# A block-sparse attention and SoLU kernel: moving VectorE's mask words into a PSUM bank, narrowing the masks, and merging TensorE's mask products

## The chip, the cores and the metric

The kernel runs on one core of a Trainium2 chip, as one launch. The metric is device time in microseconds (us). Before the change the median of three runs is 208.88 us (207.01 to 212.43). One further execution was profiled. It took 206.78 us, of which 205.1 us lie between the first and the last profiled instruction (the span).

## What is computed

The inputs are q, k and v of shape (4 batches, 8 heads, 768 tokens, 64), a table of three sampled key blocks for each of the 24 query blocks of 32 tokens, and the three weights of a feed-forward layer (512 to 1024 to 512). Cut to what matters:

```
scores = scale * q @ k.T                               # per batch and head, 768 x 768
mask   = |blk_i - blk_j| <= 1  or  blk_i in (0, 23)  or  blk_j in (0, 23)  or  blk_j in sampled[blk_i]
attn   = softmax(where(mask, scores, -1e9))
x      = attn @ v                                      # heads side by side: 3072 x 512
h      = x @ w_in                                      # 3072 x 1024
solu   = h * softmax(h)
out    = layer_norm(solu) * g_ln @ w_out               # 3072 x 512
```

The first and the last query block see every key. So the mask is all true in the rows of these two blocks, whatever was sampled.

## The kernel before, in words

**Tiling.** The scores are made transposed: keys on the 128 partitions, queries along the free axis. Tokens are dealt out to chunks of 128 so that a chunk holds every second token of the first 256 (chunks 0 and 1) or every fourth token of the other 512 (chunks 2 to 5). In a chunk of the first kind a block of 32 tokens is 16 neighbouring columns, in one of the second kind 8. The first query block is thus the first 16 columns of the first two query chunks, and the last query block is the last 8 columns of the last four.

A **pass** `ps` is one batch and one pair of query chunks (`j` = 0, 1, 2): 12 passes. In a pass there are four pairs of heads and, for each, three **units** `s`, each with two key chunks: 144 units in all. A unit is the work between two steps of this chain:

- `score_one` (L719): TensorE writes scores of two heads x two key chunks x 256 queries to `sco`, a pair of PSUM banks, of which there are two. TensorE works as two halves of 64 rows, called T0 and T64 in the plan: half `t` makes the scores of head `t` and owns bank `t` of the pair.
- `exps` (L740): ScalarE takes the exponential of the whole pair of banks (128 x 1024) into `exs` in SBUF.
- the mask, in one of three ways, picked by a letter in the string `MASK` (L254) for each unit. For `P` (52 units: 19 with j = 0 and 33 with j > 0) TensorE adds a product `sel x mrow` to the scores, so that masked scores are very negative: one more 256-column product for each of the two key chunks and each half, four in a unit. For `V` (28 units: 9 with j = 0 and 19 with j > 0) VectorE, and for `G` (64 units: 20 and 44) GpSimd, clears the masked values of `exs` after the exponential, in `mask_out` (L711): one instruction of 128 x 512 int32 words, each word two bf16 values, against the tile `seenV` or `seenG`, which is broadcast over heads, key chunks and query chunks. These tiles lie in SBUF and hold 64 words for each of the four cases (first key chunks or later ones, first query chunks or later ones).
- `outs_one` (L748): TensorE multiplies `exs` by V into `op`: 16 products of 65 columns in a unit, 8 for each half (the 65th column is the softmax sum). `op` is one PSUM bank, of which 2 x 2 x 65 = 260 of the 512 fp32 columns are used. Products of the two halves must not write one bank at the same time, so `half_mm` (L341) puts a wait between the last product of one half and the first of the other.
- `normalise` (L759), after three units: VectorE takes reciprocals of the sums and writes the normalised output to `xb`. The next pair of heads uses `op` after that.

After a pass, `xb` is transposed, `h_one` multiplies by w_in into the banks `h0` and `h1`, ScalarE takes exponentials (`e_half`, L840), VectorE multiplies (`solu_half`, L848), makes statistics, and after a transposing DMA `o_one` multiplies by w_out into the bank `o`. With `sco` 2 x 2, `op`, `h0`, `h1` and `o`, all 8 banks of PSUM are used.

**Order of the work.** All of this is put down as jobs by `at` (L474), with planned durations (`D_MUL` for VectorE's mask, `D_MULG` for GpSimd's, `D_SC` for one score product). `LANES` (L355) holds, by hand, the order of the jobs for each engine: T0, T64, A (ScalarE), V (VectorE), G (GpSimd), SP (DMA queue). `emit` (L481) plays the jobs through in planned time and then issues all instructions in order of planned start. So the order on VectorE, ScalarE, GpSimd and SP is the written one. TensorE has one queue, into which T0 and T64 are merged by planned start, part by part: products of different jobs interleave there, and an instruction that waits holds all behind it. `port=True` on a job says that VectorE and GpSimd may not run at the same time in the plan. The semaphores between engines are put in by the framework, from which tile each instruction reads and writes, in the order in which they are issued.

**Other lines that the change touches.** `turn_pe` (L663), `x_turn_pe` (L780) and `ln_turn_pe` (L863) use the `op` bank for transposes in the prologue and at the end. `seen_mm` (L1118) makes the mask of the four cases in a PSUM tile, and `seen_put` (L1126) turns it into `seenG` and `seenV`, with one VectorE instruction for each.

Of the kernel before, what the change touches and what calls it, by code (L numbers as in the profile page):

```python
# [8 lines left out]
FP32 = mybir.dt.float32  # L9
BF16 = mybir.dt.bfloat16  # L10
I32 = mybir.dt.int32
AX = mybir.AxisListType
ALU = mybir.AluOpType
# [196 lines left out]
def kernel(  # L210
# [11 lines left out]
    nc = tc.nc  # L222

    B, H, S, D = q.shape
# [3 lines left out]
    TQ = 128  # L228
# [7 lines left out]
    KD = d_model // 128  # L236
    KF = d_ff // 128
# [4 lines left out]
    PC = 2  # L242
    QW = PC * TQ
# [12 lines left out]
            "PGPGVPVVPGPGGVPPGGPVGGGGGGVVGGPVGGGGGPGGPVGGPGGP")  # L256

    D_SC, D_PV, D_O, D_EXP, D_EH = 109.5, 31.2, 216, 905, 565
    D_SOLU, D_NORM, D_MUL, D_BN, D_ST, D_OT, D_RS = 675, 640, 670, 610, 570, 750, 560
    D_MULG = 1360  # L260
    PE_LAT, X_LAT = 170, 75
    HALT = 95
    UNIT = 1313.47
# [50 lines left out]
    fix = work.enter_context(tc.tile_pool(name="fix", bufs=1))  # L314
# [4 lines left out]
    QT = [fix.tile([TQ, NP, NCH, TQ], BF16, name=f"QT{i}") for i in range(2)]  # L319
    sel = fix.tile([TQ, 2, TQ], BF16, name="sel")  # L320
    mrow = fix.tile([TQ, 2, TQ], BF16, name="mrow")
    seen = {e: fix.tile([TQ, 2, 2, TQ // 2], I32, name=f"seen{e}") for e in "GV"}
    VA = [fix.tile([TQ, H, NCH, D + 1], BF16, name=f"VA{i}") for i in range(2)]

    a_st = work.enter_context(tc.tile_pool(name="a_st", bufs=8))
# [6 lines left out]
    p_op = work.enter_context(tc.tile_pool(name="p_op", bufs=1, space=bass.MemoryType.PSUM))  # L332
    p_h = work.enter_context(tc.tile_pool(name="p_h", bufs=1, space=bass.MemoryType.PSUM))
    p_o = work.enter_context(tc.tile_pool(name="p_o", bufs=1, space=bass.MemoryType.PSUM))

    SYNC = mybir.DependencyInfo(mybir.DependencyClass.Sync, mybir.DependencyReason.DATA)
    held = {}
# [323 lines left out]
    def turn_pe(b, pr, key, c0, c1, pool):  # L663
        if pool == "h0":
            tp = p_h.tile([TQ, 1024], BF16, tag="h0", name=f"tp_{key}{b}_{pr}_{c0}")
        elif pool == "h1":
            tp = p_h.tile([TQ, 1024], BF16, tag="h1", name=f"tp_{key}{b}_{pr}_{c0}")
        elif pool == "op":
            tp = p_op.tile([TQ, 1024], BF16, tag="op", name=f"tp_{key}{b}_{pr}_{c0}")
        else:  # L670
            tp = p_o.tile([TQ, 1024], BF16, tag="o", name=f"tp_{key}{b}_{pr}_{c0}")
        turned[key, b, pr, c0] = tp
        for c in range(c0, c1):
            nc.tensor.matmul(tp[:, (c - c0) * TQ : (c - c0 + 1) * TQ],  # L674
                             nat[key, b, pr, c0][:, c].rearrange("p h d -> p (h d)"), ident,
                             is_transpose=True, start=(c == c0), stop=(c == c1 - 1))
# [18 lines left out]
    box = {}  # L695
    L = NPASS - 1
    exs_of, sco_of, op_of, xb_of = {}, {}, {}, {}

    def unit(s):
        ps, r = divmod(s, SLOTS)  # L700
        pr, u = divmod(r, UP)
        b, j = divmod(ps, NPB)
        return ps, b, j, pr, u

    def by_product(s):
        return MASK[s] == "P"

    def n_scores(s):
        return 4 if by_product(s) else 2

    def mask_out(eng, s):  # L711
        ps, b, j, pr, u = unit(s)
        e = exs_of[ps, pr][:, u].bitcast(I32).rearrange("p a b (c t) -> p (a b c) t", c=PC)
        m = seen[eng][:, int(u > 0), int(j > 0)].rearrange("p (o t) -> p o t", o=1)
        (V if eng == "V" else G).tensor_tensor(  # L715
            out=e, in0=e, in1=m.broadcast_to([TQ, 4 * PC, TQ // 2]),
            op=ALU.bitwise_and if eng == "V" else ALU.mult)

    def score_one(s, t, n):  # L719
        ps, b, j, pr, u = unit(s)  # L720
        if s not in sco_of:
            sco_of[s] = p_sco.tile([TQ, 2, 512], FP32, tag="sco", name=f"sco{s}")
        m, kk = divmod(n, 2)
        p = slice(t * D, (t + 1) * D)
        c = 2 * u + kk
        if m == 0:
            kt = KT[b % 2][p, pr, c, :]
            qt = QT[b % 2][p, pr, PC * j : PC * (j + 1), :].rearrange("p c t -> p (c t)")
        else:
            kt = sel[p, int(u > 0), :]  # L730
            qt = mrow[p, int(j > 0)].rearrange("p (o t) -> p o t", o=1).broadcast_to([D, PC, TQ])
        nc.tensor.matmul(sco_of[s][:, t, kk * QW : (kk + 1) * QW], kt, qt, start=(n == 0),  # L732
                         stop=(n == n_scores(s) - 1), skip_group_check=True)

    def scores(s):
        for n in range(n_scores(s)):
# [11 lines left out]
    def outs_one(s, t, n):  # L748
        ps, b, j, pr, u = unit(s)
        if (ps, pr) not in op_of:  # L750
            op_of[ps, pr] = p_op.tile([TQ, 2, PC, D + 1], FP32, tag="op", name=f"op{s}")
        op, exs = op_of[ps, pr], exs_of[ps, pr]
        r = slice(t * D, (t + 1) * D)
        hh, ic, kk = n >> 2, n >> 1 & 1, n & 1
        half_mm(("op", ps, pr), t, 16 * UP, op[:, hh, ic, :],
                exs[r, u, hh, kk, ic * TQ : (ic + 1) * TQ],
                VA[b % 2][r, 2 * pr + hh, 2 * u + kk, :])
# [20 lines left out]
                                    in_=xb_of.pop(ps).rearrange("p c m -> p (c m)"))  # L778

    def x_turn_pe(ps):  # L780
        pool, tag = (p_op, "op") if ps == L else (p_o, "o")
        box["tpx"] = tp = pool.tile([128, PC * KD, 128], BF16, tag=tag, name=f"tpx{ps}")
        xb = xb_of.pop(ps).rearrange("p c (k e) -> p (c k) e", e=128)
        for c in range(PC * KD):
            nc.tensor.matmul(tp[:, c, :], xb[:, c, :], ident, is_transpose=True,
                             start=(c == 0), stop=(c == PC * KD - 1))
        xT_of[ps] = [mo_sb.tile([128, KD, 128], BF16, tag=f"lnT_{i}", bufs=3,
                                name=f"xT{ps}_{i}")
                     for i in range(PC)]
# [71 lines left out]
    tpl_of = {}  # L861

    def ln_turn_pe(ps, i, a, z):  # L863
        t = ps * PC + i
        if a == 0:
            lnT_of[ps, i] = [mo_sb.tile([128, KF // 2, 128], BF16, tag=f"lnT_{a}",
                                        bufs=3, name=f"lnT{t}_{a}") for a in range(2)]
            tpl_of[ps, i] = p_op.tile([128, KF, 128], BF16, tag="op", name=f"tpl{t}")
        for c in range(a, z):
            nc.tensor.matmul(tpl_of[ps, i][:, c, :], solu_of[ps, i][:, c * 128 : (c + 1) * 128],  # L870
                             ident, is_transpose=True, start=(c == 0), stop=(c == KF - 1))
# [85 lines left out]
    with tc.manual_schedule():  # L957
        V, G, A = nc.vector, nc.gpsimd, nc.scalar
# [59 lines left out]
        for r in range(NR):  # L1018
            V.tensor_scalar(out=planes[:, r + 1], in0=io_f, scalar1=samp_f[:, r : r + 1],
                            scalar2=NEG, op0=ALU.not_equal, op1=ALU.mult)  # L1020
# [103 lines left out]
                                     stop=(kk + kq == 2), skip_group_check=True)  # L1124

        def seen_put(eng):  # L1126
            V.tensor_scalar(out=seen[eng], in0=box["seen"], scalar1=-0.5,
                            scalar2=1.0 if eng == "G" else -1.0, op0=ALU.is_ge, op1=ALU.mult)

        at(2.6, "T0", seen_mm, dur=140, lat=PE_LAT + X_LAT, reads=[("M", 1)], out="sn",  # L1130
           bank=("o", "sn"))
# [48 lines left out]
        for s in range(n_units):  # L1180
# [16 lines left out]
            if not by_product(s):  # L1197
                eng = MASK[s]
                at(s + A_MUL, eng, mask_out, eng, s, dur=D_MUL if eng == "V" else D_MULG,
                   reads=[("E", s), "seen"], out=("X", s), port=eng == "V")  # L1200
                got = ("X", s)
            for t in range(2):
                if True:
# [7 lines left out]
        for b in range(1, B):  # L1211
            s0 = SLOTS * NPB * (b - 1) + (L1 if b == 1 else L2)
            n = 0
# [220 lines left out]
```

## Time and profile before

| what | value |
|---|---|
| median of three runs | 208.88 us (207.01 to 212.43) |
| profiled execution, its own time | 206.78 us |
| its span, first to last instruction | 205.1 us |
| granted TensorE clock | 1.00 |
| busy share of the span: TensorE, ScalarE, VectorE, GpSimd | 95%, 85%, 77%, 71% |

How to read it. PE is TensorE, PEld its weight loads, DVE VectorE, ACT ScalarE, POOL GpSimd, SP the queue that issues DMAs. The chain that ended last is followed back from the last instruction, at each step to what released it or to the instruction before it on its engine; its shares say which engine set the end. A group is one line of code on one engine, with its count, busy time, mean duration, and the idle time before it with what ended that. `half_mm`'s line, L346, stands for most products, so these are told apart by the tile that they write: `op`, `h`, `o`, `tpx`. The ends of products are modelled: a record of an `op` product lasts 0.19 us although the next one starts 0.03 us later. Where cost on TensorE matters, the distance between starts is read, not the duration.

### The profile page before, as it was taken

To read this page: it belongs to the slowest core of one execution; us is meant where nothing else is said; L and a number is where in the kernel's file an instruction comes from. 1 tells how busy PE (TensorE), PEld (TensorE's weight loads), DVE (VectorE), ACT (ScalarE), POOL (GpSimd) and SP (SyncE) were. 2 spreads that over 40 slices of the span, in tenths; PEclk is the share of its full clock that TensorE was granted. 3 is DMA by queue.
4 is the path that set the end of the run, shared out by engine and by line. 5 is a ranking of instruction groups with operands and counts; after the bars stand their busy time and mean duration, and the time that the engine had idled before them with its cause. 6 is when DMAs were issued, how large, how long until landed. Compare 5 with 4: busy or idle time off the path is not lost.

```text
span 205.1 us, 9410 instructions
## 1 busy us (share of the span) xinstructions
PE 195.0 (95%) x4052; PEld 153.5 (75%) x4052; DVE 157.6 (77%) x374; ACT 173.8 (85%) x254; POOL 145.9 (71%) x165
## 2 busy tenths in 40 slices
PE   7899899999999999999899999999999999999992
PEld 2478677778888788887777989888788687886451
DVE  3375644899887877978579898898988978777992
ACT  4589887998998989989799999899989889883481
POOL 6497677788866978977877769798689578651211
PEclk9999999999999999999999999999999999999999
DMA  5999998565798999999999999999976225503543
GB/s 163 333 336 277 294 367 240 122 104 118 178 211 185 245 258 253 249 164 209 144 238 272 248 223 254 214 264 159 170 200 178 54 54 157 107 0 66 167 183 109
DMA packets 74977, 39.84 MB, mean 194 GB/s; under 512 B 46900, under 2 KB 71732, under 8 KB 74932
## 3 DMA queue, kind: packets, MB, share of 16 engines
q1 hardware_dynamic: 73204, 37.50, 81.8%
q0 software_dynamic: 528, 1.05, 2.7%
q8 instruction: 32, 0.52, 1.1%
q10 hardware_dynamic: 1200, 0.66, 1.1%
q14 instruction: 13, 0.11, 0.2%
HBM read 23.07 MB, written 6.29 MB: 143 GB/s over the span
## 4 chain that ended last, share of the span: by engine, by line
PE 71%; DMA 14%; SPq 4%; POOL 4%; issue 2%; ACT 2%; DVE 1%; ACTq 0%; POOLq 0%
PE op L346 22%; PE sco L732 19%; PE h L346 12%; PE o L346 9%; DMA lnT<-solu 5%; DMA st_q<-in_q_dram 4%; DMA KT<-n_k 3%; DMA st_k<-in_k_dram 2%; SPq L641 2%; PE h L812 2%; POOL exs L715 2%; POOL n_q L622 1%; PE o L913 1%; PE tp_k L674 1%; PE tp_q L674 1%
## 5 line engine op out<-in xcount | busy, mean ns | idle before, releaser
L744 ACT ACTIVATE exs<-sco 128x1024 bf16<-128x1024 f32 x144 | 140.8, 1029 | 13.3 <-PE sco L732 11.9
L715 POOL TENSOR_TENSOR exs<-exs,seenG 128x512 int32<-128x512 int32 x64 | 81.7, 1288 | 23.6 <-ACT exs L744 23.6
L346 PE MATMUL op<-VA,exs 64*128 64x65 bf16 x2304 | 95.6, 190 | 1.2 <-issue 0.8
L346 PEld LDWEIGHTS <-exs 64*128 64x128 bf16 x2304 | 86.6, 94 | 10.8 <-issue 1.9
L732 PE MATMUL sco<-QT,KT 64*128 64x256 bf16 x576 | 81.5, 272 | 1.2 <-DMA KT<-n_k 0.8
L346 PE MATMUL h<-w_in_sb,xT 64*128 64x512 bf16 x352 | 82.5, 376 | 0.0
L346 PE MATMUL o<-w_cen_sb,lnT 64*128 64x512 bf16 x320 | 80.7, 376 | 0.3 <-DMA lnT<-solu 0.3
L732 PEld LDWEIGHTS <-KT 64*128 64x128 bf16 x576 | 38.8, 94 | 8.5 <-issue 1.9
L853 DVE TENSOR_TENSOR solu<-h,e 128x512 bf16<-128x512 f32 x48 | 32.6, 684 | 4.7 <-ACT e L844 4.4
L844 ACT ACTIVATE e<-h 128x512 bf16<-128x512 f32 x48 | 28.8, 601 | 8.5 <-PE h L346 4.4
L346 PEld LDWEIGHTS <-xT 64*128 64x128 bf16 x352 | 29.7, 93 | 5.3 <-issue 1.1
L346 PEld LDWEIGHTS <-lnT 64*128 64x128 bf16 x320 | 29.0, 93 | 4.7 <-issue 0.7
L882 DVE BATCH_NORM_STATS2 stats<-solu 128x6 f32<-128x512 bf16 x48 | 31.4, 681 | 0.1
L732 PE MATMUL sco<-mrow,sel 64*128 64x256 bf16 x208 | 28.1, 276 | 0.9 <-issue 0.9
L900 POOL TENSOR_TENSOR rstd<-vpe,mhalf 128x1 f32<-128x1 f32 x24 | 14.9, 623 | 16.7 <-DVE vpe L893 16.7
L715 DVE TENSOR_TENSOR exs<-exs,seenV 128x512 int32<-128x512 int32 x28 | 23.8, 858 | 1.7 <-ACT exs L744 1.6
L765 DVE RECIPROCAL recip_all<-op 128x4 f32<-128x4 f32 x48 | 8.6, 180 | 19.2 <-PE op L346 18.0
L766 DVE TENSOR_TENSOR xb<-op,recip_all 128x256 bf16<-128x256 f32 x48 | 20.4, 424 | 1.7
L622 POOL CAST n_q<-st_q 128x768 bf16<-128x768 f32 (+2 forms) x19 | 15.7, 843 | 4.3 <-DMA st_q<-in_q_dram 4.3
L939 DVE TENSOR_SCALAR ot<-o,rstd 128x512 f32<-128x512 f32 x20 | 14.9, 745 | 4.0 <-PE o L346 3.1
L732 PEld LDWEIGHTS <-sel 64*128 64x128 bf16 x208 | 15.4, 96 | 2.5 <-issue 1.4
L622 POOL CAST VA<-st_v 128x768 bf16<-128x768 f32 x16 | 13.6, 856 | 3.8 <-DMA st_v<-in_v_dram 3.8
(79 smaller groups left out, 133.4 us busy)
## 6 DMA issues: line engine op xcount, KB each, us to landing
out_dram<-ot SPq DMA_DIRECT2D x10, 512.0 KB, 4.0
st_k<-in_k_dram SPq DMA_DIRECT2D x16, 256.0 KB, 5.1
st_v<-in_v_dram SPq DMA_DIRECT2D x16, 256.0 KB, 4.7
st_q<-in_q_dram SPq DMA_DIRECT2D x16, 256.0 KB, 4.5
st_k<-in_k_dram SPq DMA_DIRECT2D x16, 128.0 KB, 4.9
st_v<-in_v_dram SPq DMA_DIRECT2D x16, 128.0 KB, 3.9
wf<-in_moe_w_out_dram SPq DMA_DIRECT2D x4, 512.0 KB, 9.7
st_q<-in_q_dram SPq DMA_DIRECT2D x12, 128.0 KB, 4.5
```

The source lines that it names most:

```text
L346: i = nc.tensor.matmul(out, lhsT, rhs, start=(n == 0), stop=(n == n_all - 1), skip_group_check=True, is_transpose=turn)
L622: eng.tensor_copy(out=out, in_=in_)
L715: (V if eng == "V" else G).tensor_tensor(out=e, in0=e, in1=m.broadcast_to([TQ, 4 * PC, TQ // 2]), op=ALU.bitwise_and if eng == "V" else AL ...
L732: nc.tensor.matmul(sco_of[s][:, t, kk * QW : (kk + 1) * QW], kt, qt, start=(n == 0), stop=(n == n_scores(s) - 1), skip_group_check=True)
L744: nc.scalar.activation(out=exs_of[ps, pr][:, u].rearrange("p a b c -> p (a b c)"), in_=sco_of.pop(s).rearrange("p a b -> p (a b)"), func=A ...
L765: nc.vector.reciprocal(out=recip, in_=op[:, :, :, D : D + 1])
L766: nc.vector.tensor_tensor(out=xb_of[ps][:, :, 2 * pr * D : 2 * (pr + 1) * D].rearrange("p c (h d) -> p h c d", h=2), in0=op[:, :, :, 0:D], ...
L844: nc.scalar.activation(out=e_of[ps, i][:, half * HF : (half + 1) * HF], in_=h_bank(ps, i, half), func=ACT.Exp, scale=1.0, accum_out=eh_all ...
L853: nc.vector.tensor_mul(out=solu_of[ps, i][:, c], in0=h_bank(ps, i, half), in1=e_of[ps, i][:, c])
L882: nc.vector.bn_stats(out=st_of[ps, i][:, half, :], in_=solu_of[ps, i][:, half * HF : (half + 1) * HF])
L900: nc.gpsimd.tensor_tensor(out=rstd_of[ps, i], in0=stat_of.pop((ps, i)), in1=mhalf, op=ALU.pow)
L939: eng.tensor_scalar(out=o, in0=i, scalar1=rs, scalar2=None, op0=ALU.mult)
```

## The change

Four things are changed.

- **Where VectorE's mask words lie.** The `op` bank becomes one tile, `op_bank`, that is taken once and kept for the whole kernel. The accumulators `op`, and the transposes that used the bank, become views of it. `seenV` in SBUF goes; its words lie in columns 260 to 499 of `op_bank` as `seen_v`. `seenG` stays in SBUF as `seen_g`.
- **Narrower masks.** `some(j)` gives the columns that still need a mask: 16 to 127 of each chunk for j = 0, and 0 to 119 for j > 0. The instruction of VectorE and of GpSimd thus has 8 x 56 = 448 or 8 x 60 = 480 words instead of 512. `seen_put` writes `seen_v` in two instructions, one for j = 0 and one for j > 0.
- **One mask product per half.** For `P` units the two products of 256 columns for each half become one that covers both key chunks, of 4 x 112 = 448 or 4 x 120 = 480 columns. The selector is the same for both key chunks, so nothing is lost.
- **The plan's numbers.** `D_MUL` goes from 670 to 640, `D_MULG` from 1360 to 1170, a `P` unit has three parts instead of four, and VectorE's mask job no longer excludes GpSimd. `MASK` and `LANES` are unchanged.

```diff
--- before.py
+++ after.py
@@ -256,8 +256,8 @@
             "PGPGVPVVPGPGGVPPGGPVGGGGGGVVGGPVGGGGGPGGPVGGPGGP")
 
     D_SC, D_PV, D_O, D_EXP, D_EH = 109.5, 31.2, 216, 905, 565
-    D_SOLU, D_NORM, D_MUL, D_BN, D_ST, D_OT, D_RS = 675, 640, 670, 610, 570, 750, 560
-    D_MULG = 1360
+    D_SOLU, D_NORM, D_MUL, D_BN, D_ST, D_OT, D_RS = 675, 640, 640, 610, 570, 750, 560
+    D_MULG = 1170
     PE_LAT, X_LAT = 170, 75
     HALT = 95
     UNIT = 1313.47
@@ -319,7 +319,7 @@
     QT = [fix.tile([TQ, NP, NCH, TQ], BF16, name=f"QT{i}") for i in range(2)]
     sel = fix.tile([TQ, 2, TQ], BF16, name="sel")
     mrow = fix.tile([TQ, 2, TQ], BF16, name="mrow")
-    seen = {e: fix.tile([TQ, 2, 2, TQ // 2], I32, name=f"seen{e}") for e in "GV"}
+    seen_g = fix.tile([TQ, 2, 2, TQ // 2], I32, name="seen_g")
     VA = [fix.tile([TQ, H, NCH, D + 1], BF16, name=f"VA{i}") for i in range(2)]
 
     a_st = work.enter_context(tc.tile_pool(name="a_st", bufs=8))
@@ -334,6 +334,11 @@
     p_o = work.enter_context(tc.tile_pool(name="p_o", bufs=1, space=bass.MemoryType.PSUM))
 
 
+
+    op_bank = p_op.tile([TQ, 512], FP32, name="op_bank")
+    OPW = 2 * PC * (D + 1)
+    MW = TQ // 2 - 4
+    seen_v = op_bank[:, OPW : OPW + 4 * MW].bitcast(I32).rearrange("p (k j q) -> p k j q", k=2, j=2)
 
     SYNC = mybir.DependencyInfo(mybir.DependencyClass.Sync, mybir.DependencyReason.DATA)
     held = {}
@@ -666,7 +671,7 @@
         elif pool == "h1":
             tp = p_h.tile([TQ, 1024], BF16, tag="h1", name=f"tp_{key}{b}_{pr}_{c0}")
         elif pool == "op":
-            tp = p_op.tile([TQ, 1024], BF16, tag="op", name=f"tp_{key}{b}_{pr}_{c0}")
+            tp = op_bank.bitcast(BF16)
         else:
             tp = p_o.tile([TQ, 1024], BF16, tag="o", name=f"tp_{key}{b}_{pr}_{c0}")
         turned[key, b, pr, c0] = tp
@@ -706,31 +711,42 @@
         return MASK[s] == "P"
 
     def n_scores(s):
-        return 4 if by_product(s) else 2
+        return 3 if by_product(s) else 2
+
+    def some(j):
+        return (TQ // 8, TQ) if j == 0 else (0, TQ - TQ // 16)
 
     def mask_out(eng, s):
         ps, b, j, pr, u = unit(s)
+        a, z = some(j)
         e = exs_of[ps, pr][:, u].bitcast(I32).rearrange("p a b (c t) -> p (a b c) t", c=PC)
-        m = seen[eng][:, int(u > 0), int(j > 0)].rearrange("p (o t) -> p o t", o=1)
+        e = e[:, :, a // 2 : z // 2]
+        kk, kq = int(u > 0), int(j > 0)
+        m = seen_v[:, kk, kq, 0 : (z - a) // 2] if eng == "V" else seen_g[:, kk, kq, a // 2 : z // 2]
         (V if eng == "V" else G).tensor_tensor(
-            out=e, in0=e, in1=m.broadcast_to([TQ, 4 * PC, TQ // 2]),
+            out=e, in0=e, in1=m.rearrange("p (o t) -> p o t", o=1).broadcast_to(
+                [TQ, 4 * PC, (z - a) // 2]),
             op=ALU.bitwise_and if eng == "V" else ALU.mult)
 
     def score_one(s, t, n):
         ps, b, j, pr, u = unit(s)
         if s not in sco_of:
             sco_of[s] = p_sco.tile([TQ, 2, 512], FP32, tag="sco", name=f"sco{s}")
-        m, kk = divmod(n, 2)
         p = slice(t * D, (t + 1) * D)
-        c = 2 * u + kk
-        if m == 0:
+        o = sco_of[s][:, t, :]
+        if n < 2:
+            c = 2 * u + n
             kt = KT[b % 2][p, pr, c, :]
             qt = QT[b % 2][p, pr, PC * j : PC * (j + 1), :].rearrange("p c t -> p (c t)")
+            o = o[:, n * QW : (n + 1) * QW]
         else:
+            a, z = some(j)
             kt = sel[p, int(u > 0), :]
-            qt = mrow[p, int(j > 0)].rearrange("p (o t) -> p o t", o=1).broadcast_to([D, PC, TQ])
-        nc.tensor.matmul(sco_of[s][:, t, kk * QW : (kk + 1) * QW], kt, qt, start=(n == 0),
-                         stop=(n == n_scores(s) - 1), skip_group_check=True)
+            qt = mrow[p, int(j > 0), a:z].rearrange("p (o t) -> p o t", o=1).broadcast_to(
+                [D, 2 * PC, z - a])
+            o = o.rearrange("p (c t) -> p c t", t=TQ)[:, :, a:z]
+        nc.tensor.matmul(o, kt, qt, start=(n == 0), stop=(n == n_scores(s) - 1),
+                         skip_group_check=True)
 
     def scores(s):
         for n in range(n_scores(s)):
@@ -748,7 +764,7 @@
     def outs_one(s, t, n):
         ps, b, j, pr, u = unit(s)
         if (ps, pr) not in op_of:
-            op_of[ps, pr] = p_op.tile([TQ, 2, PC, D + 1], FP32, tag="op", name=f"op{s}")
+            op_of[ps, pr] = op_bank[:, 0:OPW].rearrange("p (h c e) -> p h c e", h=2, c=PC)
         op, exs = op_of[ps, pr], exs_of[ps, pr]
         r = slice(t * D, (t + 1) * D)
         hh, ic, kk = n >> 2, n >> 1 & 1, n & 1
@@ -778,8 +794,11 @@
                                     in_=xb_of.pop(ps).rearrange("p c m -> p (c m)"))
 
     def x_turn_pe(ps):
-        pool, tag = (p_op, "op") if ps == L else (p_o, "o")
-        box["tpx"] = tp = pool.tile([128, PC * KD, 128], BF16, tag=tag, name=f"tpx{ps}")
+        if ps == L:
+            tp = op_bank.bitcast(BF16).rearrange("p (c t) -> p c t", t=128)
+        else:
+            tp = p_o.tile([128, PC * KD, 128], BF16, tag="o", name=f"tpx{ps}")
+        box["tpx"] = tp
         xb = xb_of.pop(ps).rearrange("p c (k e) -> p (c k) e", e=128)
         for c in range(PC * KD):
             nc.tensor.matmul(tp[:, c, :], xb[:, c, :], ident, is_transpose=True,
@@ -865,7 +884,7 @@
         if a == 0:
             lnT_of[ps, i] = [mo_sb.tile([128, KF // 2, 128], BF16, tag=f"lnT_{a}",
                                         bufs=3, name=f"lnT{t}_{a}") for a in range(2)]
-            tpl_of[ps, i] = p_op.tile([128, KF, 128], BF16, tag="op", name=f"tpl{t}")
+            tpl_of[ps, i] = op_bank.bitcast(BF16).rearrange("p (c t) -> p c t", t=128)
         for c in range(a, z):
             nc.tensor.matmul(tpl_of[ps, i][:, c, :], solu_of[ps, i][:, c * 128 : (c + 1) * 128],
                              ident, is_transpose=True, start=(c == 0), stop=(c == KF - 1))
@@ -1124,8 +1143,15 @@
                                      stop=(kk + kq == 2), skip_group_check=True)
 
         def seen_put(eng):
-            V.tensor_scalar(out=seen[eng], in0=box["seen"], scalar1=-0.5,
-                            scalar2=1.0 if eng == "G" else -1.0, op0=ALU.is_ge, op1=ALU.mult)
+            if eng == "G":
+                V.tensor_scalar(out=seen_g, in0=box["seen"], scalar1=-0.5, scalar2=1.0,
+                                op0=ALU.is_ge, op1=ALU.mult)
+                return
+            for kq in range(2):
+                a, z = some(kq)
+                V.tensor_scalar(out=seen_v[:, :, kq, 0 : (z - a) // 2],
+                                in0=box["seen"][:, :, kq, a // 2 : z // 2], scalar1=-0.5,
+                                scalar2=-1.0, op0=ALU.is_ge, op1=ALU.mult)
 
         at(2.6, "T0", seen_mm, dur=140, lat=PE_LAT + X_LAT, reads=[("M", 1)], out="sn",
            bank=("o", "sn"))
@@ -1197,7 +1223,7 @@
             if not by_product(s):
                 eng = MASK[s]
                 at(s + A_MUL, eng, mask_out, eng, s, dur=D_MUL if eng == "V" else D_MULG,
-                   reads=[("E", s), "seen"], out=("X", s), port=eng == "V")
+                   reads=[("E", s), "seen"], out=("X", s), port=False)
                 got = ("X", s)
             for t in range(2):
                 if True:
```

## The prediction

> **What bounds the kernel now.** I read the page first: busy shares, the chain that ended last, and the costly groups.
>
> ```profile
> PE 195.0 (95%) x4052; PEld 153.5 (75%) x4052; DVE 157.6 (77%) x374; ACT 173.8 (85%) x254; POOL 145.9 (71%) x165
> ...
> PE 71%; DMA 14%; SPq 4%; POOL 4%; issue 2%; ACT 2%; DVE 1%; ACTq 0%; POOLq 0%
> ...
> L744 ACT ACTIVATE exs<-sco 128x1024 bf16<-128x1024 f32 x144 | 140.8, 1029 | 13.3 <-PE sco L732 11.9
> L715 POOL TENSOR_TENSOR exs<-exs,seenG 128x512 int32<-128x512 int32 x64 | 81.7, 1288 | 23.6 <-ACT exs L744 23.6
> ...
> L715 DVE TENSOR_TENSOR exs<-exs,seenV 128x512 int32<-128x512 int32 x28 | 23.8, 858 | 1.7 <-ACT exs L744 1.6
> ```
>
> TensorE is the bound: 71% of the chain is its own work, and where ScalarE idles before an exponential it waits for TensorE's scores (11.9 of 13.3 us). VectorE has 1% of the chain and GpSimd 4%. Next, busy time by stage, and the chain's shares by line:
>
> ```profile
> 40.00:80.00 40.00, 40.00 (x903) 32.83 (x898) 33.56 (x75) 37.56 (x55) 31.64 (x34) 1.00 0.93 187
> ```
>
> ```profile
> by line: PE op L346 22.4%; PE sco L732 18.7%; PE h L346 11.7%; PE o L346 9.3%; DMA lnT<-solu 4.7%; DMA st_q<-in_q_dram 4.3%; DMA KT<-n_k 3.0%; DMA st_k<-in_k_dram 2.1%; SPq L641 2.1%; issue 2.0%; PE h L812 1.7%; POOL exs L715 1.6%; POOL n_q
> ```
>
> In the middle of the kernel TensorE (first pair of numbers) is busy for 40.00 of 40 us and ScalarE (fourth) for 37.56. Neither has much to give back: a hole in TensorE's work there is mostly lost.
>
> **Part 1: the mask words in op's bank.** The question is what happens when VectorE reads columns 260 to 499 of a bank while TensorE accumulates in columns 0 to 259. Before, no mask touches that bank, so the two overlap freely. Whether the program lets two engines touch one bank at once, I read at the end of the kernel, where it has two such cases. First, the two halves of `tpx` are copied out by two engines into two different tiles:
>
> ```profile
> 187.97 0.75 DVE L939 TENSOR_SCALAR ot<-o,rstd 128x512 f32<-128x512 f32 x1
> ...
> 187.98 0.62 PE L785 MATMUL tpx<-ident,xb 128*128 128x128 bf16 x8
> ...
> 188.63 0.58 ACT L620 COPY xT<-tpx 128x512 bf16<-128x512 bf16 x1
> ...
> 189.25 0.42 DVE L622 COPY xT<-tpx 128x512 bf16<-128x512 bf16 x1 [0.52 <-ACT xT L620]
> ```
>
> VectorE was free at 188.72 and `tpx` finished at 188.60, yet its copy starts at 189.25, 0.04 us after ScalarE's copy of the other half ended. Second, `tpl` is written in two halves by TensorE:
>
> ```profile
> 194.18 0.39 PE L870 MATMUL tpl<-ident,solu 128*128 128x128 bf16 x4
> ...
> 195.03 0.58 ACT L620 COPY lnT<-tpl 128x512 bf16<-128x512 bf16 x1
> ...
> 195.66 0.38 PE L870 MATMUL tpl<-ident,solu 128*128 128x128 bf16 x4 [0.22 <-ACT lnT L620]
> ```
>
> The second half, other columns, waits for ScalarE's copy of the first (end 195.61) and starts 0.05 us later. So in this program engines take turns on one PSUM tile, even on disjoint columns. `op_bank` makes accumulators and mask words one such tile. I conclude that each V mask will wait for the `op` products issued ahead of it, and the `op` products issued behind it will wait for the mask; behind those, in TensorE's one queue, everything else waits too: scores (and so ScalarE), `h`, `o`. The Trainium skill, "PSUM — Partial Sum Buffer", section "PSUM bank collisions raise a hardware error", states the rule behind such waits: two engines on one bank and the same 32 partitions collide whichever columns they touch, so semaphores must guard by bank, not by address. The two waits above agree with it. By that rule the sum below stands; if only shared columns had to be ordered, the second rival's sum would.
>
> How often do the two meet? I took a stretch of 0.64 us (the new mask's length, below) from the start of each of the 28 V masks, and asked how long `op` products run in it:
>
> ```profile
> 12.83:13.47 0.64, 0.54 (x18) 0.00 (x0) 1.00 1.08 327
> ...
> 21.40:22.04 0.64, 0.09 (x3) 0.09 (x1) 1.00 1.23 208
> ...
> 29.91:30.55 0.64, 0.00 (x0) 0.00 (x0) 1.00 1.13 341
> ...
> 174.02:174.66 0.64, 0.58 (x19) 0.00 (x0) 1.00 0.00 0
> sum 17.92, PE 11.43 DVE 0.49; mean PE 0.41 DVE 0.02
> ```
>
> Sixteen stretches are like the first and the last, with `op` at work for over 0.5 us from the start on; eight have between 0.09 and 0.41 us (1.96 us in all); four have at most 0.01. One of the sixteen, and what a hand-over costs:
>
> ```profile
> 73.84 0.47 PE L346 MATMUL op<-VA,exs 64*128 64x65 bf16 x10
> ...
> 74.10 0.68 DVE L715 TENSOR_TENSOR exs<-exs,seenV 128x512 int32<-128x512 int32 x1
> ...
> 74.24 0.23 PE L346 MATMUL op<-VA,exs 64*128 64x65 bf16 x2
> ```
>
> ```profile
> L346 PE MATMUL op<-VA,exs x2304: 187/191/202, 12.4 to 186.9; 64*128 64x65 bf16 x192
> ```
>
> ```profile
> 13.93 0.41 PE L346 MATMUL op<-VA,exs 64*128 64x65 bf16 x8
> ...
> 14.37 0.18 DVE L765 RECIPROCAL recip_all<-op 128x4 f32<-128x4 f32 x1 [0.65 <-PE op L346]
> ```
>
> Ten products whose records span 0.47 us start 0.03 us apart. In the hand-over to VectorE the reciprocal starts 0.03 us after the last record ends, so about 0.23 us after that product's start (0.19 + 0.03). So a mask in mid-burst costs TensorE's queue 0.23 (product to mask) + 0.64 (mask) + 0.05 (mask to product, as with `tpl`) less the usual 0.03: 0.89 us. Sixteen are 14.2 us. The eight partial ones cost at least the product time that is pushed behind the mask, 1.96, and 0.05 each: 2.4. Sum 16.6 us. Bounds: 11.4 (only the overlap in the sum row is pushed back) and 28 x 0.92 = 25.8 (every mask in mid-burst). What of it reaches the end? The chain is TensorE's for 71%; the rest is DMA and others, under which a hole is hidden. 0.71 x 16.6 = **+11.8 us**. VectorE's own wait lies beside its idle time (23% of the span), but `solu_half` and `normalise` are queued behind it, which I leave to the upper bound.
>
> **Part 2: what the masks cost by themselves.** No mask with a PSUM operand is in the trace. The nearest row is the product of `h` (PSUM) with `e` (SBUF); a smaller one gives the slope.
>
> ```profile
> L853 DVE TENSOR_TENSOR solu<-h,e x48: 672/681/693, 33.7 to 197.3; 128x512 bf16<-128x512 f32 x48
> ```
>
> ```profile
> L715 POOL TENSOR_TENSOR exs<-exs,seenG x64: 1259/1268/1779, 16.7 to 183.8; 128x512 int32<-128x512 int32 x64
> L715 DVE TENSOR_TENSOR exs<-exs,seenV x28: 672/701/1556, 12.8 to 174.0; 128x512 int32<-128x512 int32 x28
> ```
>
> ```profile
> L766 DVE TENSOR_TENSOR xb<-op,recip_all 128x256 bf16<-128x256 f32 x48 | 20.4, 424 | 1.7
> ```
>
> (681 - 424) / 256 = 1.0 ns a column: 448 columns take 617 ns and 480 take 649; with 9 and 19 masks the mean is 0.64 us. The old mask has a tail (median 701, most 1556) and so has GpSimd's (1268, 1779), while `solu`, which reads one operand from PSUM, has none. So I take the tail as gone: 28 x (858 - 640) = 6.1 us of VectorE. GpSimd's mask goes by columns from its shortest: 1102 and 1180, mean 1156 with 20 and 44; 64 x (1288 - 1156) = 8.4 us. VectorE's gain lies beside TensorE's work (1% of the chain) and counts nothing; if that cover went, it would be up to 6.1. Of GpSimd's 81.7 us, 1.6% of the span, 3.3 us, lie on the chain; a tenth of that is saved: **-0.3 us**, bounds 0 and -3.3.
>
> **Part 3: one mask product per half.**
>
> ```profile
> 29.26 0.27 PE L732 MATMUL sco<-QT,KT 64*128 64x256 bf16 x1
> ...
> 29.37 0.27 PE L732 MATMUL sco<-QT,KT 64*128 64x256 bf16 x1
> ...
> 29.48 0.27 PE L732 MATMUL sco<-mrow,sel 64*128 64x256 bf16 x1
> ...
> 29.59 0.27 PE L732 MATMUL sco<-mrow,sel 64*128 64x256 bf16 x1
> ```
>
> Products of 256 columns start 0.11 us apart: 0.42 ns a column. With j = 0 a unit saves 64 columns (27 ns) in each half, with j > 0, 32 (13 ns). The halves run side by side, so one counts: 19 x 27 + 33 x 13 = 0.94 us, times 0.71: **-0.7 us**. The 104 instructions that go away are worth at most 0.03 us each, the distance of `op` starts: 3.1 us as the bound; other work starts in between, so I take nothing for them.
>
> **Part 4: the rest.**
>
> ```profile
> L1127 DVE TENSOR_SCALAR seenV<-seen_ps 128x256 int32<-128x256 f32 x1 | 0.4, 412 | 0.0
> ```
>
> ```profile
> L622 DVE CAST mrow<-m_ps 128x128 bf16<-128x128 f32 x2 | 0.6, 285 | 0.2 <-PE m_ps L1028 0.2
> ```
>
> `seen_put` for VectorE becomes two instructions of 112 and 120 columns; by the 128-column cast they take up to 0.57 us instead of 0.41. This one time, 0.16 us is hidden under TensorE's prologue; uncovered it costs 0.16. The changed numbers of the plan move where T0's and T64's products interleave; the plan counts the merged product as 109.5 ns, by the rows above it is 0.19 to 0.20. I give this 0, with 1 us to either side.
>
> **The sum.** 206.8 (profiled execution) + 11.8 - 0.3 - 0.7 = 217.6 us. The median of the runs before is 2.1 us above the profiled one, so a median after may lie between 217.6 and 219.7; I say **218.5**. The likeliest case's own range goes with 7.5 to 17 us of added time: 213 to 225.
>
> **Rivals.**
>
> - *The holes grow.* Each V mask ties three engines in a row: TensorE waits for the mask, the mask for the exponential, the exponential for scores that TensorE makes. For it: ScalarE's 37.56 of 40 us leave little to catch up. Against it: two `sco` buffers. All 16.6 us count, and in the four idle and eight partial stretches the masks move into bursts too (25.8 at most): 206.8 + 16.6 to 25.8 - 1 gives 222 to 232, middle 227. Chance 0.17.
> - *No turns are taken, not slower.* Accumulators and mask words are views of one tile, but are ordered only where columns overlap. Place: the same 28 masks; price: zero instead of 16.6. It decides as soon as TensorE starts `op` products during a mask. Then only the gains are left: -0.3 - 0.7, with up to -3.3 and -3.1 as bounds: 203 to 206, middle 205.5. For it: the prologue and the end are the only places where the trace shows turns. Against it: both show them on disjoint columns. Chance 0.13, of which faster by over 2% 0.04.
> - *VectorE waits, not TensorE.* If the order of issue puts most masks just behind a burst of `op`, TensorE loses little and VectorE's waits (28 x about 0.5 = 14 us) go into its 47 idle us. For it: four stretches without `op`. Against it: sixteen with. 206.8 + 2.4 to 6, less 1: 208 to 212. Chance 0.15, half of it within 2%.
> - *The forecast*: chance 0.55.
>
> 2%, 4.1 us, is about what a measurement of this kernel can tell from no change. Slower by more: 0.55 + 0.17 + 0.07 = 0.79. Faster by more: 0.04. Within: 0.17. The range for 8 in 10 reaches from the lower end of the third rival, 208, to just past the middle of the first, 228; what lies outside is the second rival (0.13) and a tail of the first.
>
> **What would show it.** Right: among the waits, VectorE's masks wait for `op` products, and `op` products or their weight loads wait for `exs` L715, some 24 times and 0.5 to 0.9 us each; in the stretch of a mask no `op` product starts; ScalarE's wait for `sco` grows from 11.9 us by a similar sum; V masks take 0.62 to 0.65 us without tail, GpSimd's mean falls to about 1.16 us; merged products, half as many, are followed 0.19 to 0.20 us later by the next of their half. Wrong: `op` products that start while a mask reads the bank; or the waits are there and the time is not, because TensorE catches up.

## The result and the profile after

The kernel after takes 221.51 us (median of six runs, 221.0 to 222.1), the kernel before 209.26 us (six runs, 207.01 to 212.43). The ratio is 1.0626, with a 95% interval of 1.0561 to 1.069: slower by 12.3 us. Medians are over all runs and ratios over the fast ones: some runs of the kernel before, and of the kernels below that come out like it, are over 1.5% slower than their fastest, so a loss taken from medians is a little too small (between medians of fast runs it is 12.6 us here, and 14.0 where 13.4 is named below). The forecast was 218.5 us in a range of 208 to 228, slower with a chance of 0.79. The profiled execution after took 221.24 us, with a span of 219.7 us.

First the page after, with the rows that answer to those of before: busy time, the chain by engine and by line, and the groups of ScalarE's exponential, of `op`'s products (now `op_bank`) and of the two kinds of mask.

```profile
PE 197.3 (90%) x3948; PEld 150.3 (68%) x3948; DVE 153.3 (70%) x375; ACT 174.9 (80%) x254; POOL 134.1 (61%) x165
...
PE 82%; DVE 9%; ACT 2%; DMA 2%; issue 2%; SPq 0%; DVEq 0%; ACTq 0%
PE op_bank L351 29%; PE sco L748 19%; PE h L351 13%; PE o L351 11%; DVE exs L726 7%; DMA st_k<-in_k_dram 2%; PE h L831 2%; PE tpx L351 1%; PE o L932 1%; PE tp_q L679 1%; ACT exs L760 1%; PE mean_ps L1184 1%; PE oo L932 1%; PE tp_k L679 1%; DVE xb L782 1%
...
L760 ACT ACTIVATE exs<-sco 128x1024 bf16<-128x1024 f32 x144 | 141.1, 1027 | 22.8 <-PE sco L748 20.2
L351 PE MATMUL op_bank<-VA,exs 64*128 64x65 bf16 x2304 | 97.0, 190 | 13.5 <-DVE exs L726 13.4
L726 POOL TENSOR_TENSOR exs<-exs,seen_g 128x480 int32<-128x480 int32 (+1 forms) x64 | 75.0, 1181 | 51.1 <-ACT exs L760 51.1
...
L726 DVE TENSOR_TENSOR exs<-exs,op_bank 128x480 int32<-128x480 int32 (+1 forms) x28 | 17.9, 640 | 11.5 <-PE op_bank L351 10.7
```

Every engine's share of the span has fallen: all wait more. TensorE's busy time has even grown, from 195.0 to 197.3 us, with 104 products fewer. All of VectorE was 1% of the chain; now its mask alone is 7% of the span on it (15 us). The idle time ahead of `op` products was 1.2 us before and is 13.5 us now, and 13.4 of it ends with VectorE's mask. ScalarE's wait for scores has grown from 11.9 to 20.2 us.

The waits say it in both directions. The columns are the total in us, the number of times, and the longest.

```profile
ACT exs L760 <- PE sco L748: 20.2, 29, 1.6
PEld L351 <- issue: 19.6, 28, 1.2
...
PE op_bank L351 <- DVE exs L726: 13.4, 21, 0.8
DVE exs L726 <- PE op_bank L351: 10.7, 20, 1.2
```

The busy time of `op` products (and of the few transposes in that bank) inside the V masks, each cut by 0.02 us at its start and to 0.58 us:

```profile
13.17:13.75 0.58, 0.00 (x0) 1.00 1.13 317
...
186.66:187.24 0.58, 0.00 (x0) 1.00 0.91 184
sum 16.23, PE 0.00; mean PE 0.00
```

Before, 11.43 of 17.92 us of mask time had `op` products under it. Now it is 0.00 of 16.23, in all 28. The two never run at once. TensorE as a whole does not always stand: with other products it is busy for 6.21 of these 16.23 us; in 12 of the 28 masks it does nothing.

One of the turns from near, the same unit that the prediction showed at 74.10 us:

```profile
77.57 0.36 PE L748 MATMUL sco<-mrow,sel 64*128 64x480 bf16 x1
...
77.77 0.63 PE L351 MATMUL op_bank<-VA,exs 64*128 64x65 bf16 x15
...
78.51 0.66 DVE L726 TENSOR_TENSOR exs<-exs,op_bank 128x480 int32<-128x480 int32 x1 [0.25 <-PE op_bank L351]
79.22 0.19 PE L351 MATMUL op_bank<-VA,exs 64*128 64x65 bf16 x1 [0.82 <-DVE exs L726]
...
79.23 0.39 PE L351 MATMUL h<-w_in_sb,xT 64*128 64x512 bf16 x1
...
79.25 0.38 PE L748 MATMUL sco<-QT,KT 64*128 64x256 bf16 x2
```

The 15 products end at 78.40, the mask runs from 78.51 to 79.17, and the next product starts at 79.22. Behind that one product stand an `h` product and two score products, which have nothing to do with the bank; they come 0.01 to 0.03 us after it. That is the queue behind the wait. In the middle of the kernel it leaves TensorE 36.69 busy us of 40, where it had 40.00:

```profile
40.00:80.00 40.00, 36.69 (x804) 28.66 (x800) 30.59 (x69) 34.70 (x50) 29.71 (x34) 1.00 0.87 183
```

### The profile page after: what moved, and what is told of

Same layout as the page of the kernel before. It is cut to its first block, busy times and chain, and to the rows that moved or that the text cites. A ratio compares the mean times of both kernels' runs of the same rounds, so it can differ in the third digit from the quotient of the medians.

```text
span 219.7 us, 9199 instructions
## 1 busy us (share of the span) xinstructions
PE 197.3 (90%) x3948; PEld 150.3 (68%) x3948; DVE 153.3 (70%) x375; ACT 174.9 (80%) x254; POOL 134.1 (61%) x165
## 4 chain that ended last, share of the span: by engine, by line
PE 82%; DVE 9%; ACT 2%; DMA 2%; issue 2%; SPq 0%; DVEq 0%; ACTq 0%
PE op_bank L351 29%; PE sco L748 19%; PE h L351 13%; PE o L351 11%; DVE exs L726 7%; DMA st_k<-in_k_dram 2%; PE h L831 2%; PE tpx L351 1%; PE o L932 1%; PE tp_q L679 1%; ACT exs L760 1%; PE mean_ps L1184 1%; PE oo L932 1%; PE tp_k L679 1%; DVE xb L782 1%
## 5 line engine op out<-in xcount | busy, mean ns | idle before, releaser
L760 ACT ACTIVATE exs<-sco 128x1024 bf16<-128x1024 f32 x144 | 141.1, 1027 | 22.8 <-PE sco L748 20.2
L351 PE MATMUL op_bank<-VA,exs 64*128 64x65 bf16 x2304 | 97.0, 190 | 13.5 <-DVE exs L726 13.4
L726 POOL TENSOR_TENSOR exs<-exs,seen_g 128x480 int32<-128x480 int32 (+1 forms) x64 | 75.0, 1181 | 51.1 <-ACT exs L760 51.1
L351 PEld LDWEIGHTS <-exs 64*128 64x128 bf16 x2304 | 87.6, 94 | 27.0 <-issue 18.4
L748 PE MATMUL sco<-QT,KT 64*128 64x256 bf16 x576 | 83.0, 271 | 0.4 <-ACT exs L760 0.3
L863 ACT ACTIVATE e<-h 128x512 bf16<-128x512 f32 x48 | 28.8, 600 | 10.7 <-PE h L351 7.3
L748 PE MATMUL sco<-mrow,sel 64*128 64x480 bf16 (+1 forms) x104 | 27.5, 367 | 0.0
L781 DVE RECIPROCAL recip_all<-op_bank 128x4 f32<-128x4 f32 x48 | 8.7, 181 | 25.4 <-PE op_bank L351 24.1
L726 DVE TENSOR_TENSOR exs<-exs,op_bank 128x480 int32<-128x480 int32 (+1 forms) x28 | 17.9, 640 | 11.5 <-PE op_bank L351 10.7
L919 POOL TENSOR_TENSOR rstd<-vpe,mhalf 128x1 f32<-128x1 f32 x24 | 13.2, 553 | 18.9 <-DVE vpe L912 18.4
L782 DVE TENSOR_TENSOR xb<-op_bank,recip_all 128x256 bf16<-128x256 f32 x48 | 20.4, 424 | 1.7
L627 POOL CAST n_k<-st_k 128x768 bf16<-128x768 f32 x15 | 12.3, 824 | 4.1 <-DMA st_k<-in_k_dram 4.1
L627 POOL CAST n_q<-st_q 128x768 bf16<-128x768 f32 (+2 forms) x19 | 13.3, 713 | 1.8 <-DMA st_q<-in_q_dram 1.8
```

What stands on the lines that cost most here:

```text
L351: i = nc.tensor.matmul(out, lhsT, rhs, start=(n == 0), stop=(n == n_all - 1), skip_group_check=True, is_transpose=turn)
L627: eng.tensor_copy(out=out, in_=in_)
L726: (V if eng == "V" else G).tensor_tensor(out=e, in0=e, in1=m.rearrange("p (o t) -> p o t", o=1).broadcast_to([TQ, 4 * PC, (z - a) // 2]), ...
L748: nc.tensor.matmul(o, kt, qt, start=(n == 0), stop=(n == n_scores(s) - 1), skip_group_check=True)
L760: nc.scalar.activation(out=exs_of[ps, pr][:, u].rearrange("p a b c -> p (a b c)"), in_=sco_of.pop(s).rearrange("p a b -> p (a b)"), func=A ...
L781: nc.vector.reciprocal(out=recip, in_=op[:, :, :, D : D + 1])
```

## The experiments

The theory is that of the prediction: one tile for the whole bank makes VectorE's masks and `op` products take turns, and TensorE's queue stands still meanwhile. The rivals are that the merged products or the changed order of issue cost the time, that holding the bank as one tile costs something whoever reads it, and that only the hand-overs or only the mask's length counts. Eight kernels were run in two groups. Each group shares runs of the kernel before, whose median is 209.71 us in the first and 209.5 us in the second. Numbers are medians, ratios are to the kernel before.

**All words back in SBUF.** The changed kernel, but:

```diff
-    seen_v = op_bank[:, OPW : OPW + 4 * MW].bitcast(I32).rearrange("p (k j q) -> p k j q", k=2, j=2)
+    seen_v = fix.tile([TQ, 2, 2, MW], I32, name="seen_v")
```

> The changed kernel with one thing undone: VectorE's mask words lie in a tile of their own in SBUF (the same narrow words), so no mask touches op's bank. Theory (engines take turns on the bank): all of the loss goes, and what is left is the small gain of the narrow masks and merged products: 1 us less than before, from 3 less to no change (about 206 to 209 us where before is 209). Rival (the merged products or the changed order of issue cost the time): it stays above 215 us.

Measured: 208.06 us (206.01 to 209.6), ratio 0.9967 (0.9904 to 1.003). One line of placement carries the whole loss, 221.5 - 208.1 = 13.4 us; the narrow masks, merged products, single `op_bank` tile and the plan's numbers are all still in this kernel and cost nothing that shows. TensorE's wait for masks is no longer among its waits. ScalarE's wait for scores (20.2 us in the kernel after) and the time in which TensorE's weight loads wait for nothing that the profile shows ("issue", 19.6 us) have fallen too. The first line is the busy time:

```profile
PE 195.4 (95%) x3948; PEld 150.7 (73%) x3948; DVE 155.3 (76%) x375; ACT 173.9 (85%) x254; POOL 139.2 (68%) x165
...
ACT exs L760 <- PE sco L748: 7.9, 20, 1.2
...
PEld L351 <- issue: 5.7, 12, 1.5
```

**Two mask products again, words in the bank.** The changed kernel with `n_scores` back at 4 for P units, each product covering one key chunk:

```diff
-        return 3 if by_product(s) else 2
+        return 4 if by_product(s) else 2
...
-                [D, 2 * PC, z - a])
-            o = o.rearrange("p (c t) -> p c t", t=TQ)[:, :, a:z]
+                [D, PC, z - a])
+            o = o[:, kk * QW : (kk + 1) * QW].rearrange("p (c t) -> p c t", t=TQ)[:, :, a:z]
```

> The changed kernel with the merged mask product undone: two products of 224 or 240 columns for each half again, words still in the bank. Theory: as after or up to 2 us slower (221.5 to 223.5 us), since the loss is the turns. Rival (one long product delays the other half and the scores behind it): it falls by more than 4 us, below 217.

Measured: 222.87 us (221.92 to 224.1), ratio 1.072 (1.06 to 1.084). The loss stays: the merged product is not its cause.

**Nine of the 28 masks in the bank.** The words for j > 0 go to a tile in SBUF (`seen_put` writes them there), those for j = 0 stay:

```diff
+    seen_w = fix.tile([TQ, 2, MW], I32, name="seen_w")
...
-        m = seen_v[:, kk, kq, 0 : (z - a) // 2] if eng == "V" else ...
+        m = (seen_w[:, kk] if kq else seen_v[:, kk, kq, 0 : (z - a) // 2]) if eng == "V" else ...
```

> The changed kernel with only the words for j = 0 in op's bank (9 of the 28 masks); the other 19 masks read a tile in SBUF. Theory: the loss goes with the number of masks that read the bank, 9/28 of some 13 us: 4 us above the kernel with all words in SBUF, 2 to 6. Rival (the bank held as one tile costs a fixed time, whoever reads it): 10 us or more above it.

Measured: 212.26 us (211.88 to 212.93), ratio 1.0214 (1.0113 to 1.0314): 4.2 us above the kernel with all words in SBUF, where 9/28 of 13.4 us are 4.3. Its waits follow:

```profile
PE op_bank L352 <- DVE exs L727: 5.8, 8, 0.8
...
DVE exs L727 <- PE op_bank L352: 4.5, 8, 0.7
```

The loss goes by the number of masks that read the bank. A fixed part of 10 us is excluded; one of a microsecond or two would not show, as the interval of the ratio is 2 us to either side.

**Short masks in the bank.** VectorE's mask works on 64 words instead of 448 or 480, which leaves the mask of the V units incomplete:

```diff
+        if eng == "V":
+            a, z = a, a + 16
         e = e[:, :, a // 2 : z // 2]
```

> The changed kernel in which VectorE's mask works on the first 16 columns (8 words) of each chunk only, so 64 words instead of 448 or 480; this leaves the mask of the 28 V units incomplete. The words stay in the bank. By the rows of before a mask then takes about 0.23 us instead of 0.64. Theory: a turn costs 0.23 (product to mask) + 0.23 + 0.05 - 0.03 = 0.48 us instead of 0.89, so about half of the 12 us loss goes: 213 to 218 us. Rival (what costs is the mask's length alone): 209 to 212. Rival (what costs is that a wait exists, whatever its length): 219 to 222.

Measured: 212.74 us (212.3 to 214.98), ratio 1.0263 (1.0136 to 1.039). A mask now takes 0.22 us.

```profile
L728 DVE TENSOR_TENSOR exs<-exs,op_bank x28: 208/220/222, 12.6 to 178.1; 128x64 int32<-128x64 int32 x28
```

```profile
DVE exs L728 <- PE op_bank L351: 11.0, 19, 1.2
...
PE op_bank L351 <- DVE exs L728: 5.0, 14, 0.4
```

The median is 0.3 us short of the range expected of the theory and 0.7 us above that of the first rival, so it lies in neither; the second rival (219 to 222) falls. Of the 13.4 us 4.7 remain, a share of 0.35, with masks 0.34 as long. So the time alone goes with the mask's length, and does not show what the hand-overs cost. That they are still there is seen in the waits: VectorE waits 11.0 us for products, against 10.7, and TensorE's 14 waits come to 5.0 us, where 14 masks are 3.1 us.

**Each mask twice.** The second mask clears the same bits:

```diff
-        (V if eng == "V" else G).tensor_tensor(
+        for _ in range(2 if eng == "V" else 1):
+            (V if eng == "V" else G).tensor_tensor(
...
```

> The changed kernel with each of VectorE's 28 masks issued twice in a row (the second changes nothing, as it clears the same bits). A turn is longer by 0.64 us. Theory (each microsecond of a mask in the bank is a hole in TensorE's queue, for the 16 masks in mid-burst and, now, most of the eight partial ones): 16 to 24 x 0.64 us more, of which 0.71 to 1 arrive: 7 to 15 us above after, 228.5 to 236.5 us. Rival (only the hand-overs cost, or TensorE catches up): less than 4 us above it.

Measured: 244.77 us (242.66 to 246.28), ratio 1.1794 (1.1656 to 1.1932): 23.3 us above the kernel after, beyond the 15 us that the theory allowed at most.

```profile
L727 DVE TENSOR_TENSOR exs<-exs,op_bank x56: 611/653/655, 12.5 to 209.8; 128x480 int32<-128x480 int32 x38, 128x448 int32<-128x448 int32 x18
```

```profile
PE 201.9 (84%) x3944; PEld 153.1 (63%) x3948; DVE 171.0 (71%) x403; ACT 176.0 (73%) x254; POOL 134.2 (56%) x165
```

```profile
ACT exs L761 <- PE sco L749: 37.1, 38, 2.7
PE op_bank L351 <- DVE exs L727: 31.8, 28, 1.7
```

TensorE now waits for all 28 masks and by 18.4 us more (31.8 - 13.4), about the 28 x 0.65 = 18.2 us by which the masks grew. Hardly any of that is absorbed, and another 5 us is on top. In the profiled execution the span is 21.5 us longer than in the kernel after: TensorE is idle for 16.9 us more (39.3 us instead of 22.4, the span less the busy time) and busy for 4.6 us more with the same products. So what is on top is busy time, not more holes. The prediction's first rival, holes that grow into each other, is not what shows here: ScalarE's wait for scores goes from 20.2 to 37.1 us, but a mask hardly ever waits for an exponential (once, 0.8 us). The granted clock was 0.7 in three of the 40 slices of this run, but its mean, 0.979, is close to the 0.983 of the kernel after. What lengthens the busy time stays open.

**A plan that knows of the turns.** Words in the bank; in `emit`, no `op` job starts in planned time while a V mask runs, and the other way round:

```diff
...
         def can(j, now):
+            if j["fn"] is outs_one and turn["V"] > now:
+                return False
+            if j["fn"] is mask_out and j["eng"] == "V" and turn["T"] > now:
+                return False
...
+                    if who:
+                        turn[who] = max(turn[who], end + (PE_LAT if who == "T" else X_LAT))
...
```

> The changed kernel, with words in the bank, but the plan is told of the turns: in planned time no op product job starts while a V mask runs, and no V mask while an op job runs, with 170 and 75 ns between them. The order of jobs on each lane stays; where T0's and T64's products interleave changes. Theory: the turns stay, and with them most of the loss, since a lane whose next job is an op job waits anyway; but the other half's scores, h and o products are now issued ahead of the wait and fill part of the hole: 213 to 219 us. Rival (the third of the prediction: what matters is whether the mask comes in mid-burst; placed behind whole jobs VectorE waits instead and TensorE loses little): 208 to 212. Rival (lanes in a fixed order leave nothing to fill in): 220 or more.

Measured: 216.99 us (216.26 to 217.85), ratio 1.0444 (1.0328 to 1.0559).

```profile
DVE exs L737 <- PE op_bank L351: 11.3, 15, 1.4
...
PE op_bank L351 <- DVE exs L737: 1.3, 5, 0.4
```

```profile
PE 202.8 (94%) x3944; PEld 151.7 (71%) x3948; DVE 152.3 (71%) x375; ACT 175.4 (82%) x254; POOL 134.5 (63%) x165
```

The visible holes are all but gone (1.3 us), and yet only 4.5 of 13.4 us come back. The same products now keep TensorE busy for 202.8 us instead of 197.3: with one half's next job barred, the other half's products run alone where two ran side by side. That reading fits the busy time; the records don't name the half, so it is argued, not shown. The prediction's third rival (VectorE waits instead, 208 to 212) falls: VectorE waits as long as before, and TensorE still loses.

**Two further looks at the small terms.** The merged product alone on the kernel before:

```diff
-        return 4 if by_product(s) else 2
+        return 3 if by_product(s) else 2
...
```

> The kernel before with one part of the change alone: one narrow mask product per half for P units instead of two (and three planned parts instead of four). VectorE's and GpSimd's masks stay full and in SBUF. Prediction's term: 0.7 us less (bounds 0 and 3.1). Rival (the merged product, planned at 109.5 ns and really longer, upsets the interleave): 1 to 4 us more.

Measured: 207.72 us (204.94 to 211.94), ratio 0.993 (0.9836 to 1.0024). The rival is excluded beyond 0.5 us; a gain of 0.7 us can't be told from none.

And the kernel with words in SBUF, with the plan keeping VectorE's masks and GpSimd apart again:

```diff
-                   reads=[("E", s), "seen"], out=("X", s), port=False)
+                   reads=[("E", s), "seen"], out=("X", s), port=eng == "V")
```

> The kernel with all words in SBUF, narrow masks and merged products (the one that came out at 208.06 us), and the plan again keeps VectorE's masks and GpSimd apart, with GpSimd's mask planned as 1200 ns. If the two engines' collisions (VectorE's longest mask 1544 ns where the median is 648) cost time on the path, this is 1 to 3 us faster, 205 to 207 us; if they lie beside TensorE's work, as the prediction had it, it is the same within 1 us.

Measured: 207.5 us (204.94 to 211.6), ratio 0.9969 (0.9904 to 1.0033): 0.6 us below the kernel without, within the 1 us that was said for no cost on the path. But the plan did not keep the two engines apart in the run: their masks still overlap for 3.6 us in all, where it was 3.8 us without. VectorE's longest mask is still 1446 ns (1544 without), and GpSimd's 1726 (1735):

```profile
L726 POOL TENSOR_TENSOR exs<-exs,seen_g x64: 1127/1202/1726, 17.0 to 181.7; 128x480 int32<-128x480 int32 x44, 128x448 int32<-128x448 int32 x20
L726 DVE TENSOR_TENSOR exs<-exs,seen_v x28: 607/648/1446, 12.1 to 171.8; 128x480 int32<-128x480 int32 x19, 128x448 int32<-128x448 int32 x9
```

So what the collisions cost stays open. No kernel without turns is clear of the kernel before.

## Why the prediction was right

- **The mechanism.** Right, and shown by four kernels: the loss goes when the words leave the bank, scales with the number of masks in it, and falls and grows with their length. Which rule of the framework or the chip asks for the turns was not tried. It could be read off before the change, from two waits at the end of the kernel on disjoint columns of one tile.
- **The size of a turn.** The mask's length was right: 640 ns as forecast, 608 to 655. So was mask to product, 0.05 us. Product to mask was set at 0.23 us, counted from the last product's start. In the turn shown it is 0.30 (the last of 15 records, 0.19 us long, ends at 78.40, and the mask starts at 78.51): a full turn costs some 0.07 us more than the 0.89 that was reckoned.
- **How many turns.** I counted 24 masks that would make TensorE wait; 21 waits ended with a mask.
- **The sum.** The raw holes were put at 16.6 us, from start to start of products. The profile's 13.4 us count idle time from the end of the last record, which is 0.19 us after its start; less the usual 0.03, that is 13.4 + 21 x 0.16 = 16.8 us, an estimate. The total was right, its parts less so: 21 waits with 0.80 us of hole on average, where sixteen of 0.89 and eight of 0.30 were reckoned. The term that was mis-sized is the factor 0.71, the chain's share of TensorE: 13.4 us of loss from 16.8 us of holes is 0.80, so 11.8 us should have been 13.4. And the share of the chain is not the right measure: TensorE was busy for 95% of the span before, so it was at work also for most of the time in which the chain ran through DMAs (14%), and had little idle time to hide a hole in. The profiled executions show where the loss lies (us; idle is the span less the busy time):

  | kernel | span | TensorE busy | idle | of it waits for masks | other idle |
  |---|---|---|---|---|---|
  | words in SBUF | 205.4 | 195.4 | 10.0 | 0 | 10.0 |
  | nine in the bank | 210.1 | 196.0 | 14.1 | 5.8 | 8.3 |
  | short masks | 210.6 | 195.5 | 15.1 | 5.0 | 10.1 |
  | after | 219.7 | 197.3 | 22.4 | 13.4 | 9.0 |
  | each mask twice | 241.2 | 201.9 | 39.3 | 31.8 | 7.5 |
  | the plan knows | 215.0 | 202.8 | 12.2 | 1.3 | 10.9 |

  Of the 13.4 us of waits only 1.0 is hidden in other idle time, and TensorE's busy time adds 1.9 us. In the last two kernels it adds 6.5 and 7.4 us, which the holes alone would not have told. Of the 3.0 us by which 218.5 was short, 1.6 lie in this term and about as much in the base: 207.7 us was taken, and the six runs before have the median 209.26.
- **The gains.** -0.3 and -0.7 us were forecast; the kernel that has all of them and no turns is at -0.7 us (ratio 0.9967, from -2.0 to +0.6 us). The sum agrees within that; the terms are too small to be told apart.
- **The tails.** VectorE's longest mask fell from 1556 to 655 ns and GpSimd's from 1779 to 1215, as forecast from `solu`'s rows. GpSimd's mean is 1181 ns, not 1156: its cost goes down by less than the columns.
- **The signs.** No `op` product ran in a mask, as said. ScalarE's wait for scores grew by 8.3 us, where a sum like that of the holes was said: less than their 13.4. A merged product is followed after 0.20 us by the first `op` product (77.57 to 77.77), as said.

## What to carry to other kernels

Spare columns in a PSUM bank are not spare room: in this program a tile there takes turns with whatever accumulates in the bank, and 21 of the 28 reads became a stop in TensorE's queue. Before moving an operand, look in the trace for an existing pair of engines on one tile but different columns; whether the second waits answers the question. At an engine that bounds the kernel, count the holes nearly in full, not by the engine's share of the chain: of 13.4 us of waits 12.4 were added to TensorE's idle time. Then compare its busy time as well, since filling the holes by another order of issue lengthened it by 5.5 us and won back only a third.

## What the runs showed of the hardware that was not expected

The tails of the two masks come from VectorE and GpSimd both reading SBUF, and not from the masks' width. Narrow masks with words in SBUF still have them, and lose them with words in PSUM. First the kernel with words in SBUF, then the kernel after (min, median, max in ns):

```profile
L726 POOL TENSOR_TENSOR exs<-exs,seen_g x64: 1129/1204/1735, 17.5 to 184.0; 128x480 int32<-128x480 int32 x44, 128x448 int32<-128x448 int32 x20
L726 DVE TENSOR_TENSOR exs<-exs,seen_v x28: 606/648/1544, 13.3 to 174.2; 128x480 int32<-128x480 int32 x19, 128x448 int32<-128x448 int32 x9
```

```profile
L726 POOL TENSOR_TENSOR exs<-exs,seen_g x64: 1127/1201/1215, 17.5 to 196.8; 128x480 int32<-128x480 int32 x44, 128x448 int32<-128x448 int32 x20
L726 DVE TENSOR_TENSOR exs<-exs,op_bank x28: 608/644/655, 13.2 to 186.6; 128x480 int32<-128x480 int32 x19, 128x448 int32<-128x448 int32 x9
```

The Trainium skill, "SBUF — State Buffer", section "Who interferes with whom", says that a VectorE instruction with two inputs from SBUF contends with a GpSimd instruction that reads SBUF, and one with at most one such input, outside the modes in which VectorE uses two ports, does not; the rows agree. Nor is the tail gone because the two engines no longer meet: in the kernel after GpSimd is busy for 9.48 of the 16.23 us inside VectorE's masks. What the move freed was real. With words in SBUF VectorE's masks are busy for 15.9 + 5.6 us, against 17.9 us in the kernel after:

```profile
L726 DVE TENSOR_TENSOR exs<-exs,seen_v 128x480 int32<-128x480 int32 x19 | 15.9, 843 | 1.1 <-ACT exs L760 1.1
L726 DVE TENSOR_TENSOR exs<-exs,seen_v 128x448 int32<-128x448 int32 x9 | 5.6, 618 | 0.4 <-ACT exs L760 0.3
```

These 3.6 us lay beside the bound, and the turns were paid on it.
